# Attention and a routed expert layer on one core: scatter writes without mutual waits, weights in parts, reordered preparation

## The chip, the cores and the metric

The program runs on one core of a Trainium2 chip. The metric is the device time of one execution in microseconds (us). The core has five instruction streams that run side by side and wait for one another by semaphores: PE (TensorE, matrix products), DVE (VectorE), ACT (ScalarE), POOL (GpSimd) and SP (which here only issues transfers). Each stream executes its instructions in the order of the program, so an instruction that waits holds up everything behind it on the same engine. In the profile, PEld stands for the loading of weights into TensorE, and a name with q (SPq, POOLq) for the queue of that engine.

## What is computed

Attention over 8 batches, 12 heads, 448 tokens and head size 64, all in fp32, and behind it a layer in which only 128 of the 448 tokens of a batch, those with the highest gate score, go through two matrix products:

```
q_n, k_n = rmsnorm(q, g_q), rmsnorm(k, g_k)
attn = softmax(scale * q_n @ k_n.T)           # per batch and head
x = (attn @ v) with the heads side by side    # (8, 448, 768)
scores = x @ w_gate
out = x.copy()
for b in range(8):
    top = indices of the 128 highest scores[b]
    h = max(x[b, top] @ w1, 0)                # w1: 768 x 1024
    out[b, top] += sigmoid(scores[b, top]) * (h @ w2)
```

## The kernel before

**Tiling.** Four heads form a group; a batch has 3 groups, the whole problem 24. The 448 keys of a group are cut into 7 units of 64, so there are 168 units. `scores(u)` (L252) makes the transposed scores of a unit for 4 heads with 64x32 tiles of the array, and ACT turns them into probabilities `p` (L261), scaled by the keys' inverse norms `rinv`. `values(u)` (L278) multiplies them with `v` into two banks `av` that gather over the 7 units of a group. `add_probs` (L291, DVE) adds the probabilities up over the units; `sum_keys` (L315, `den`) and `invert_sums` (L331, `denT`, and a reciprocal on DVE) make the softmax's denominators from that sum. `values_out` (L303 on ACT, L305 on DVE) moves the finished `av` to SBUF as `xT`, and `to_tokens` (L345, L347), once for each pair of heads, turns it to token rows `x` and divides.

**Norms.** For each group ahead of its first unit: `squares` (ACT, L167) and `sum_squares` (DVE, L173) for the queries and the keys, `rinv` by a power on POOL (L177), then `rows_out` and `rows_in` (L190, L202): the queries' `rinv` goes to DRAM and comes back spread over the partitions as `bc`, with which `scale_q` (DVE, L211) scales the queries. Group 0 takes a way through TensorE instead (`scale_q_early`, L223).

**Selection and experts.** When a batch's 3 groups are done, `gate` (DVE, L368) makes the scores, `spread` and `score_rows` lay them out as rows, `count` (DVE, L401) gives each token its rank, `annotate` adds its gate and its row number, `select` (L433) writes the rows with rank under 128 to DRAM by four indirect transfers from POOL, and `load_selected` (L447, `xe`) reads them back. `mixture(b)` is a generator of 9 pieces: a head of transposes (L463), 4 pieces of the first product (L480), 4 half pieces of the second (L497, with L506 on DVE behind each half), and an indirect write of the rows at the end (L515, POOL).

**Order.** The program's order is written out by hand. The main loop goes in steps `k` of two units: scores of units 2k and 2k+1, values of the two units before, then what stands under slot 2k in a table `todo`, one piece of the running mixture, then slot 2k+1. A group that ends in step k has its `den` and `denT` in step k+1 and both `to_tokens` in step k+2; a batch has its `select` in the second half of step k+5, the load of `xe` in step k+6 and the head of its mixture in step k+8. 21 units make 10.5 steps, so the heads of successive mixtures stand 10 or 11 steps apart, and 9 of these steps carry a piece. All loads of inputs and weights, the `rows`/`bc` transfers, the store of `x` and the load of `xe` go through SP's one queue, in program order; a transfer there also waits until the eighth one before it has landed.

## Time and profile before

| | us |
|---|---|
| median of 3 runs | 658.07 (656.1 to 661.79) |
| profiled execution, device time | 659.13 |
| its span, first to last instruction | 657.4 |
| PE busy | 546.7 (83%) |
| DVE busy | 359.4 (55%) |
| ACT busy | 276.8 (42%) |
| POOL busy | 186.4 (28%) |
| mean granted TensorE clock | 0.928 of full |

The page shows the span of one execution, the busy time of each engine and, where asked, the rows of single instructions: start and duration in us, engine, line of the kernel, what it writes and reads, and in square brackets how long the engine had been idle and what ended that. A row with xN stands for N instructions of one kind in a run. A busy PE is not PE at its peak.

### The profile page before, as it was taken

How to read it: one execution, taken by the hardware profiler on the slowest of the kernel's cores; microseconds unless marked ns; L12 is line 12 of the kernel's file. 1: busy time of each engine (PE TensorE's matmuls, PEld its weight loads, DVE VectorE, ACT ScalarE, POOL GpSimd, SP SyncE). 2: the span in 40 equal slices, each digit the busy share in tenths (PEclk: the TensorE clock that was granted, in tenths of full speed). 3: DMA queues.
4: the chain of work that ended last, by engine and by line, in shares of the span. 5: the costliest groups of instructions: out<-in, count | busy, mean ns of one | idle time of the engine just before them, and what ended most of it. 6: DMA issues, size and time to landing. Idle time of an engine off the chain costs nothing.

```text
span 657.4 us, 15932 instructions
## 1 busy us (share of the span) xinstructions
PE 546.7 (83%) x6920; PEld 282.4 (43%) x6920; DVE 359.4 (55%) x588; ACT 276.8 (42%) x497; POOL 186.4 (28%) x99
## 2 busy tenths in 40 slices
PE   1638988689997999499996999599998999797185
PEld 1213333246434554156433654256435643284182
DVE  1446879554873568454873558554876476335000
ACT  1335665544544545444543544444544544410000
POOL 2633442511154223412053232512055212100200
PEclk9959998879997999979996999989999999798589
DMA  7975556172706534272806534273706331102200
GB/s 247 397 266 169 171 197 225 41 245 104 251 22 197 195 109 169 67 236 86 253 20 205 187 91 167 68 230 112 252 27 220 113 114 35 40 1 84 72 1 28
DMA packets 46914, 93.99 MB, mean 143 GB/s; under 512 B 11510, under 2 KB 29686, under 8 KB 46836
## 3 DMA queue, kind: packets, MB, share of 16 engines
q1 hardware_dynamic: 43492, 86.58, 39.9%
q0 software_dynamic: 3200, 6.31, 2.9%
q8 instruction: 56, 0.92, 0.6%
q14 instruction: 22, 0.18, 0.1%
q10 hardware_dynamic: 144, 0.00, 0.0%
HBM read 75.39 MB, written 25.36 MB: 153 GB/s over the span
## 4 chain that ended last, share of the span: by engine, by line
PE 53%; issue 21%; DMA 10%; POOL 7%; DVE 5%; ACT 3%; POOLq 0%; SPq 0%; DVEq 0%; ACTq 0%
PE sc L252 16%; PE av L278 13%; PE moe_ps L480 10%; PE moe_ps L497 7%; POOL selected L433 4%; DMA selected<-x,rank 4%; DMA xe<-selected 4%; PE x_ps L345 3%; DMA tok<-in_tok_dram 2%; POOL rinv L177 2%; ACT p L261 2%; DVE ss L173 2%; PE den_ps L315 1%; PE denT_ps L331 1%; DVE sum L291 1%
## 5 line engine op out<-in xcount | busy, mean ns | idle before, releaser
L261 ACT ACTIVATE p<-sc,rinv 128x448 f32<-128x448 f32 x336 | 186.5, 634 | 156.8 <-PE sc L252 141.2
L177 POOL TENSOR_TENSOR rinv<-ss,neg_half 128x14 f32<-128x14 f32 x48 | 136.7, 2848 | 300.6 <-DVE ss L174 280.2
L252 PE MATMUL sc<-qT,kT 64*32 64x448 f32 x2688 | 162.8, 588 | 15.9 <-ACT p L261 11.3
L278 PE MATMUL av<-p,v 64*32 64x448 f32 x2688 | 154.1, 556 | 7.3 <-ACT xT L303 7.3
L291 DVE TENSOR_TENSOR sum<-sum,p 128x896 f32<-128x896 f32 x120 | 129.3, 1077 | 4.7
L480 PEld LDWEIGHTS moe_ps<-xeT,w 128*128 128x128 f32 x768 | 90.5, 196 | 14.9 <-ACT p L261 11.0
L480 PE MATMUL moe_ps<-xeT,w 128*128 128x128 f32 x768 | 95.4, 282 | 1.5 <-ACT hT L487 1.5
L278 PEld LDWEIGHTS av<-p,v 64*32 64x32 f32 x2688 | 54.1, 111 | 90.1 <-issue 73.1
L497 PE MATMUL moe_ps<-w,hT 128*128 128x384 f32 x256 | 91.1, 502 | 1.9 <-DVE xe L506 1.4
L252 PEld LDWEIGHTS sc<-qT,kT 64*32 64x32 f32 x2688 | 46.6, 111 | 83.9 <-issue 60.6
L173 DVE TENSOR_REDUCE ss<-sq 128x14 f32<-128x896 f32 x48 | 51.9, 1080 | 35.1 <-ACT sq L167 35.1
L433 POOL DMA_INDIRECT selected<-x,rank x32 | 38.7, 1210 | 95.0 <-DVE x L426 46.6
L497 PEld LDWEIGHTS moe_ps<-w,hT 128*128 128x128 f32 x256 | 47.1, 193 | 41.7 <-issue 10.3
L347 DVE TENSOR_TENSOR x<-x_ps,rden 112x512 f32<-112x512 f32 x48 | 33.1, 690 | 40.5 <-PE x_ps L345 39.7
L167 ACT ACTIVATE sq<-tok 128x896 f32<-128x896 f32 x48 | 46.2, 962 | 14.8 <-DMA tok<-in_tok_dram 10.2
L487 ACT ACTIVATE hT<-moe_ps 128x256 f32<-128x256 f32 x32 | 12.3, 383 | 88.4 <-PE moe_ps L480 88.4
L345 PE MATMUL x_ps<-ident,xT 128*112 128x128 f32 x192 | 30.5, 281 | 11.9 <-DVE x L347 11.5
L463 PE MATMUL moe_ps<-ident,xe 128*128 128x128 f32 x24 | 6.5, 401 | 40.7 <-DMA xe<-selected 40.7
L506 DVE SCALAR_TENSOR_TENSOR xe<-moe_ps,xe 128x384 f32<-128x384 f32 x16 | 9.9, 618 | 53.2 <-PE moe_ps L497 53.1
L211 DVE SCALAR_TENSOR_TENSOR qT<-qT,gg,bc 128x896 f32<-128x896 f32 x23 | 26.4, 1148 | 17.3 <-DMA bc<-rows 17.3
L345 PEld LDWEIGHTS x_ps<-ident,xT 128*112 128x112 f32 x192 | 20.3, 133 | 32.7 <-DVE x L347 14.0
L305 DVE COPY xT<-av 128x448 f32<-128x448 f32 x24 | 15.0, 624 | 31.0 <-PE av L278 31.0
(54 smaller groups left out, 242.5 us busy)
## 6 DMA issues: line engine op xcount, KB each, us to landing
tok<-in_tok_dram SPq DMA_DIRECT2D x48, 448.0 KB, 6.5
qT<-in_qT_dram SPq DMA_DIRECT2D x24, 448.0 KB, 5.8
kT<-in_kT_dram SPq DMA_DIRECT2D x24, 448.0 KB, 7.6
v<-in_vp_dram SPq DMA_DIRECT2D x24, 448.0 KB, 7.6
out_dram<-x SPq DMA_DIRECT2D x8, 1344.0 KB, 7.3
bc<-rows SPq DMA_DIRECT2D x46, 224.0 KB, 4.0
w<-in_moe_w_dram SPq DMA_DIRECT2D x2, 3072.0 KB, 20.6
xe<-selected SPq DMA_DIRECT2D x8, 385.0 KB, 3.2
```

The costliest lines, as they stand in the source:

```text
L167: nc.scalar.activation(out=sq, in_=t, func=AF.Square, scale=scale)
L173: nc.vector.tensor_reduce(out=ss, in_=sq, axis=AX.X, op=OP.add)
L177: nc.gpsimd.tensor_tensor(out=rinv.rearrange(flat), in0=ss.rearrange(flat), in1=neg_half.to_broadcast([128, 2 * NI]), op=OP.pow,)
L252: nc.tensor.matmul(out=scs[hh][o : o + 32, 0:S], lhsT=kTs[n][r, c, D * i + k0 : D * i + k0 + 32], rhs=qTs[n][r, c, :], start=True, stop=True,)
L261: nc.scalar.activation(out=p[:, hh], in_=scs[hh][:, 0:S], func=AF.Exp, scale=rinvs[n, 1][:, hh, i : i + 1],)
L278: nc.tensor.matmul(out=avs[n][c][o : o + 32, 0:S], lhsT=vs[n][r, hh, i, d0 : d0 + 32], rhs=probs[u][r, hh], start=(i == 0), stop=(i == NI ...
L291: nc.vector.tensor_tensor(out=sums[n], in0=probs[u - 1] if i == 1 else sums[n], in1=probs[u], op=OP.add)
L345: nc.tensor.transpose(out=ps[:CP, j, :], in_=t[:, j, :], identity=ident)
L347: nc.vector.tensor_tensor(out=xs[b][:, :, col : col + 128].rearrange("p j (h d) -> p j h d", d=D), in0=ps[:CP].rearrange("p j (h d) -> p j ...
L433: nc.gpsimd.indirect_dma_start(out=t[:, :], out_offset=bass.IndirectOffsetOnAxis(ap=rank[:, j : j + 1], axis=0), in_=x[:, j, :], in_offset ...
L480: nc.tensor.matmul(out=ps[:, 128 * i : 128 * i + n], lhsT=w1[:, dc, 128 * (f0 + i) : 128 * (f0 + i + 1)], rhs=xeT[:, dc, :n], start=(dc == 0),
L497: nc.tensor.matmul(out=ps[:n, : DM // 2], lhsT=hT[:, fc, :n], rhs=w2[:, fc, cols], start=(fc == 0), stop=(fc == NFC - 1),)
```

## The change

- `select`: the four indirect writes of a batch are declared free of each other; each had waited for the one before.
- Weights: `w1` and `w2` had been loaded whole, right behind the first loads, ahead of the keys of group 1 and the tokens of group 2. They are now loaded in 14 parts, one in each slot from 8 to 21 (steps 4 to 10).
- Preparation: the first loads come in another order, those of group 1 among them; group 1's squares, sums and `rows`/`bc` transfers are issued ahead of the first scores; squares have two buffers; a small exponential ahead of everything loads ACT's table; the constant `earlier` is filled on POOL rather than on DVE and in step 4 rather than at the start.
- Queries come as (j, p) rather than (p, j) from the host, so that `values_out` and the copy of `den` read their bank straight; both copies of `values_out` are now on ACT.
- `sum_keys` makes its sums in four column tiles of 224 columns, where it had two of 448; the copy to `den` is 128x224 rather than 64x448, and `denT` takes two transposes rather than four.
- Order: a list of `tasks` is worked off at two places in a step, ahead of and behind the piece of the mixture. A group that ends in step q has `den` behind the piece of step q, `denT` ahead of that of q+1, the first `to_tokens` behind it, the second ahead of the piece of q+2. The first unit of a group is left to the next step where the group before it ends in this one.
- `gate` works per group on 256 columns (12 pieces for a batch, and a sum), where it had 4 pieces of 768 at the batch's end. `annotate` and `select` come in the first half of step q+5, ahead of the piece of the mixture; the load of `xe` too is in step q+5; the head stays in step q+8.
- The mixture's first product fills a whole bank before it is copied (two copies rather than four); the last batch's mixture takes the four banks of the scores, where it had one. `p` has 7 buffers rather than 6.

```diff
-    def load_weights():
-        nc.sync.dma_start(out=wg, in_=_bcast_row(moe_w_gate, CP))
-        nc.sync.dma_start(out=w1, in_=moe_w1.rearrange("(c p) f -> p c f", p=128))
-        nc.sync.dma_start(out=w2, in_=moe_w2.rearrange("(c p) f -> p c f", p=128))
+    def load_w(part):
+        if part == 0:
+            nc.sync.dma_start(out=wg, in_=_bcast_row(moe_w_gate, CP))
+        for w, src in ((w1, moe_w1), (w2, moe_w2)):
+            n = w.shape[1]
+            if part < n:
+                nc.sync.dma_start(
+                    out=w[:, part], in_=src.rearrange("(c p) f -> p c f", p=128)[:, part]
+                )
...
+            for odd in range(2):
+                o = 64 * odd + 32 * hh
+                nc.tensor.matmul(
+                    out=ps[o : o + 32, 0 : S // 2],
...
-            w = nc.gpsimd.indirect_dma_start(
+            for other in writes:
+                tc.declare_no_dep(w.ins, other.ins, reason="different rows")
+            writes.append(w)
...
+        def bank():
+            if b == B - 1:
+                return ps_sc.tile([128, 512], F32, name="sc")
+            return ps_moe.tile([128, 512], F32, tag="moe", name="moe_ps")
...
+    for part in range(NDC + NFC):
+        at(8 + part, load_w, part)
+    at(9, constants)
...
+        task((q, 1), sum_keys, n)
+        task((q, 2) if HALVES > 1 else (q + 1, 0), invert_sums, n)
+        task((q + 1, 0) if HALVES > 1 else (q + 1, 1), to_tokens, n, 0)
+        task((q + 1, 1) if HALVES > 1 else (q + 2, 0), last_tokens, n)
...
+        s = PER * (now[0] + 1)
+        at(s, count, b, (0, 1))
+        at(s + 1, count, b, (2, 3))
+        at(s + 2, annotate, b)
+        at(s + 2, select, b)
+        at(s + 3, load_selected, b)
+        ready.append((b, (s + 3) // PER + 4 // HALVES - 1))
```

(HALVES is 1 and PER is 2.)

Three places show what moves. The first is POOL's stream at the selection of the third batch: `selected` are the four indirect writes, `rinv` a norm ahead of them, and what a row waits for stands in brackets, where DMASW with a number is one of the eight completion semaphores that POOL's transfers take in turn, DMAHW the same for SP's, and the others stand for an engine. Before:

```order
L177 TENSOR_TENSOR rinv<-ss,neg_half 128x14 [waits DVE_49,Activation_49]
L433 DMA selected<-x,rank 128x770 [waits DVE_49]
L433 DMA selected<-x,rank 128x770 [waits DMASW3_49,DMASW2_49]
L433 DMA selected<-x,rank 128x770 [waits DMASW3_49]
L433 DMA selected<-x,rank 128x770 [waits DMASW4_49]
```

And of the change:

```order
L191 TENSOR_TENSOR rinv<-ss,neg_half 128x14 [waits DMAHW3_49,DMAHW4_49,DVE_49,Pool_49]
L454 DMA selected<-x,rank 128x770 [waits DMASW1_49,DVE_49]
L454 DMA selected<-x,rank 128x770 [waits DMASW2_49]
L454 DMA selected<-x,rank 128x770 [waits DMASW3_49]
L454 DMA selected<-x,rank 128x770 [waits DMASW4_49]
```

Before, the semaphore is that of the write just ahead; in the change each write takes the semaphore that a write of an earlier batch had used eight transfers back, and waits for that one alone.

The second place is SP's stream from its first load on. Before, with `w_143` and `w_144` for the two weights:

```order
L91 DMA tok<-in_tok_dram 128x896
L91 DMA qT<-in_qT_dram 128x2x448
L91 DMA tok<-in_tok_dram 128x896
L91 DMA kT<-in_kT_dram 128x2x448
L91 DMA v<-in_vp_dram 128x896
L91 DMA tok<-in_tok_dram 128x896 x2
L91 DMA qT<-in_qT_dram 128x2x448
L158 DMA wg<-in_moe_w_gate_dram 112x768
L159 DMA w_143<-in_moe_w_dram 128x6x1024
L160 DMA w_144<-in_moe_w_dram 128x8x768
L91 DMA kT<-in_kT_dram 128x2x448
L91 DMA v<-in_vp_dram 128x896
```

And of the change:

```order
L92 DMA tok<-in_tok_dram 128x896 x2
L92 DMA qT<-in_qT_dram 128x2x448
L92 DMA kT<-in_kT_dram 128x2x448
L92 DMA tok<-in_tok_dram 128x896 x2
L92 DMA v<-in_vp_dram 128x896
L92 DMA qT<-in_qT_dram 128x2x448
L92 DMA kT<-in_kT_dram 128x2x448
L92 DMA v<-in_vp_dram 128x896
L204 DMA rows<-rinv 64x2x7 x2
L216 DMA bc<-rows 64x2x448 x2
L92 DMA tok<-in_tok_dram 128x896 x2
```

The weights are gone from the start; the last row, the tokens of group 2, now stands behind the `rows` and `bc` of group 1, which wait for POOL.

The third place is PE's stream around the end of the second group, where no mixture runs. Before:

```order
L315 MATMUL den_ps<-sum,pick_pair 32x448 x2
L331 MATMUL denT_ps<-ident,den 112x64 x4
L252 MATMUL sc<-qT,kT 32x448 x16
L278 MATMUL av<-p,v 32x448 x16
L345 MATMUL x_ps<-ident,xT 112x128 x8
L252 MATMUL sc<-qT,kT 32x448 x16
```

And of the change:

```order
L327 MATMUL den_ps<-sum,pick_pair 32x224 x4
L266 MATMUL sc<-qT,kT 32x448 x16
L292 MATMUL av<-p,v 32x448 x16
L345 MATMUL denT_ps<-ident,den 112x128 x2
L359 MATMUL x_ps<-ident,xT 112x128 x4
L266 MATMUL sc<-qT,kT 32x448 x16
L292 MATMUL av<-p,v 32x448 x16
L359 MATMUL x_ps<-ident,xT 112x128 x4
```

Scores and values now stand between `den` and `denT` and between the two `x_ps`, which share one bank.

## Rows read from the trace of the kernel before

**Rows 1.** Stretches: length, busy time (instructions) per engine, granted clock, DMA share, GB/s.
```profile
20.00:40.00 20.00, 8.65 (x145) 3.83 (x144) 5.62 (x10) 8.28 (x14) 9.57 (x8) 0.86 1.04 400
50.50:124.70 74.20, 61.86 (x1036) 23.59 (x1028) 56.03 (x86) 45.93 (x80) 28.04 (x12) 0.95 0.50 168
55.50:86.60 31.10, 26.95 (x488) 10.49 (x480) 23.70 (x31) 20.68 (x36) 13.22 (x4) 1.00 0.45 147
132.70:567.20 434.50, 397.08 (x5148) 204.07 (x5148) 263.08 (x426) 203.68 (x369) 128.50 (x63) 0.95 0.45 144
495.80:567.20 71.40, 65.95 (x890) 33.87 (x890) 43.30 (x69) 33.06 (x61) 17.92 (x9) 1.00 0.36 114
567.20:621.80 54.60, 36.42 (x262) 23.45 (x262) 17.16 (x38) 6.61 (x14) 4.72 (x5) 0.81 0.15 48
```

**Rows 2.** Waits: engine, line, releaser: total us, times, longest us.
```profile
PE moe_ps L463 <- DMA xe<-selected: 40.7, 8, 14.1
```

**Rows 3.** Timeline of PE at two heads of a mixture.
```profile
270.08 1.72 PE L252 MATMUL sc<-qT,kT 64*32 64x448 f32 x32
...
273.23 0.95 PE L315 MATMUL den_ps<-sum,pick_pair 128*32 128x448 f32 x4
279.35 0.91 PE L463 MATMUL moe_ps<-ident,xe 128*128 128x128 f32 x3 [5.17 <-DMA xe<-selected]
...
282.06 3.24 PE L252 MATMUL sc<-qT,kT 64*32 64x448 f32 x32
...
291.28 1.74 PE L252 MATMUL sc<-qT,kT 64*32 64x448 f32 x32
...
555.23 0.65 PE L345 MATMUL x_ps<-ident,xT 128*112 128x128 f32 x4 [0.78 <-DVE x L347]
...
559.65 0.99 PE L278 MATMUL av<-p,v 64*32 64x448 f32 x16 [1.35 <-ACT xT L303]
...
567.21 0.90 PE L463 MATMUL moe_ps<-ident,xe 128*128 128x128 f32 x3 [2.69 <-DMA xe<-selected]
```

**Rows 4.** The tile selected: issue on POOL, ns min/median/max; then landing.
```profile
L433 POOL DMA_INDIRECT selected<-x,rank x32: 940/943/2407, 117.4 to 615.6; - x32
...
DMA to landing us min/median/max: 2.5/2.9/5.0
```

**Rows 5.** Timeline of POOL at the last selection.
```profile
606.57 0.94 POOL L433 DMA_INDIRECT selected<-x,rank  x1 [44.16 <-DVE x L426]
...
615.58 0.94 POOL L433 DMA_INDIRECT selected<-x,rank  x1 [2.04 <-DMA selected<-x,rank]
616.82 0.96 POOL L515 DMA_INDIRECT out_dram<-xe,row  x1 [0.30 <-issue]
```

**Rows 6.** Timeline of DVE and ACT in the opening stretch.
```profile
17.50 1.08 DVE L173 TENSOR_REDUCE ss<-sq 128x14 f32<-128x896 f32 x1
...
37.70 0.95 ACT L167 ACTIVATE sq<-tok 128x896 f32<-128x896 f32 x1 [10.24 <-DMA tok<-in_tok_dram]
...
44.79 1.15 DVE L211 SCALAR_TENSOR_TENSOR qT<-qT,gg,bc 128x896 f32<-128x896 f32 x1 [2.70 <-DMA bc<-rows]
```

**Rows 7.** DMA issues: queue, count, KB each, median us from issue to landing.
```profile
tok<-in_tok_dram SPq DMA_DIRECT2D x48, 448.0 KB, 6.5
...
rows<-rinv SPq DMA_DIRECT2D x46, 3.5 KB, 2.7
```

**Rows 8.** Timeline of DVE at the last batch's ranks.
```profile
601.61 0.62 DVE L506 SCALAR_TENSOR_TENSOR xe<-moe_ps,xe 128x384 f32<-128x384 f32 x1 [5.04 <-PE moe_ps L497]
```

**Rows 9.** Groups by line: busy us, mean ns, idle before.
```profile
L177 POOL TENSOR_TENSOR rinv<-ss,neg_half 128x14 f32<-128x14 f32 x48 | 136.7, 2848 | 300.6 <-DVE ss L174 280.2 <-issue 8.5 <-DMA v<-in_vp_dram 7.2
...
L480 PE MATMUL moe_ps<-xeT,w 128*128 128x128 f32 x768 | 95.4, 282 | 1.5 <-ACT hT L487 1.5
...
L368 DVE SCALAR_TENSOR_TENSOR prod<-x,wg 112x768 f32<-112x768 f32 x32 | 30.6, 955 | 0.8
...
masks.py:197 POOL MEMSET ident<- 128x128 f32 x1 | 0.2, 204 | 3.9 <-DVEq L1084 3.9
```

More of the change, by code (lines that the diff above doesn't have):

```diff
@@ new lines, in run_values @@
+    def run_values(upto, q):
+        ended = False
+        while waiting and waiting[0] <= upto:
+            u = waiting[0]
+            if ended and u % NI == 0:
+                return
+            values(waiting.pop(0))
+            if u % NI == NI - 1:
+                values_out(u // NI)
+                finish(u // NI, q)
+                ended = True
+            add_probs(u)
+    sq = {}
+    sq[0, 0] = squares(0, 0)
+    sum_squares(0, 0, sq.pop((0, 0)))
+    sq[0, 1] = squares(0, 1)
@@ new lines, in fast @@
+    sum_squares(0, 1, sq.pop((0, 1)))
+    sq[1, 0] = squares(1, 0)
+    sq[1, 1] = squares(1, 1)
+    scale_q_early(0)
+    sum_squares(1, 0, sq.pop((1, 0)))
+    rows_out(1)
+    sum_squares(1, 1, sq.pop((1, 1)))
+    rows_in(1)
+    waiting = list(range(units))
+    moe, ready, done, q = iter(()), [], 0, 0
+    while done < B:
+        now[0] = q
+        for half in range(HALVES):
+            k = 2 * (HALVES * q + half)
+            for u in (k, k + 1):
+                if u < units:
+                    scores(u)
+            run_values(k - 1, q)
+            for slot in (k, k + 1):
+                for fn in todo.pop(slot, ()):
+                    fn()
+        opening(q, 0)
+        for half in range(HALVES):
+            end = next(moe, None)
+            if end is None and ready and q >= ready[0][1]:
+                moe = mixture(ready.pop(0)[0])
+                end = next(moe)
+                done += 1
+            opening(q, half + 1)
+            if end and HALVES > 1:
+                break
+        q += 1
```

206 lines of the change are left out of this document (94 added, 112 removed).

## The prediction

> **What bounds the kernel now.** I read the stretches first, then the waits, then the single rows at the places that the two name. The span falls into four parts: up to the head of the first mixture at 132.7 us; six batches from there to 567.2, 434.5 us; the last batch's way to its selected rows, 54.6 us; and its mixture, 35.6 us, from 621.8 to the end at 657.4 [rows 1]. In the third of these that is clean, 495.8 to 567.2, PE is busy 65.95 of 71.4 us at a granted clock of 1.00, and DVE 43.30: with a mixture running, PE is the bound. Where it isn't busy, the waits name one cause above all: the first transpose of a mixture waits for `xe`, 40.7 us in 8 waits, the longest 14.1 [rows 2]; the other seven make 26.6, 3.8 each. Behind such a wait PE pays again: after 5.17 us of waiting the scores of two units take 3.24 us, where 1.74 is the time a few steps later [rows 3], the two clock levels of 1.2 and 2.4 GHz. The opening is another thing: there one square on ACT sits 10.24 us for tokens that stand behind both weights in SP's queue [rows 6].
>
> **The change, part by part.**
>
> **The opening.** With the weights away, the tokens of group 2 wait for something else: SP has the `rows` and `bc` of group 1 ahead of them, and `rows` needs POOL. DVE gets to the sum for group 1's queries at about 17.0 (17.50 in [rows 6], less half a microsecond for the table that is loaded earlier); 1.2 for the sum and its small follower, 2.8 for the power [rows 9], 2.7 for `rows` to land and 6.5 for `bc` and tokens behind it [rows 7] make 30.2, where the square started at 37.70. That is 7.5 us. The wait of 2.70 for group 1's `bc` [rows 6] goes too, since it is issued ahead of those tokens: 10.2 in all.
>
> **Attention without a mixture.** From 55.5 to 86.6 seven steps take 31.1 us, 4.44 each, with PE busy 26.95 and DVE 23.70 [rows 1]. The new order puts scores and values between `den` and `denT` and between the two `x_ps`. PE's work falls by what four column tiles save: `den` takes 0.95 now [rows 3]; halved columns on twice the tiles can save from nothing to half, and I take 0.4 for each of the two groups. DVE loses two copies to ACT, whose 20.68 of 31.1 has room for them, and gains eight pieces of `gate`: a piece of 768 columns takes 0.955 [rows 9], one of 256 between a third of that and all of it; I take 0.5, near the third since the work is by column, which makes DVE about 26.5. So both engines end near 26.3, 3.8 a step at the least; with both that full I take 4.1, half way to 4.44. The stretch from 50.5 to 124.7 holds 15 steps in 74.2 us [rows 1]; now 61.5, plus 3 for the first batch's ranks on DVE: 64.5, a gain of 9.7.
>
> **Weights in the middle.** They are 6.3 MB in seven steps, some 29 us, beside two groups' loads of 2.7 MB each: 12 MB. From 20 to 40 us the queues moved 400 GB/s [rows 1], so 30 us are needed; I add 2 us for loads that come late. The Trainium skill, DMA: Bandwidth & Descriptors, section "Where 436 GB/s comes from", gives about 358 GB/s as the limit of HBM for one core; by that these loads would need 33.5 us, and the sum would be 3 us longer. The row has 400, and the measurement decides.
>
> **The writes of selected rows.** From the first to the last issue are 9.0 us now, 606.57 to 615.58, three turns of 3.0, of which the issue itself is 0.94 and the rest the landing of the write ahead; the next transfer behind the last of them, which waited for none of these, came 1.24 after it [rows 5]. Four issues in a row so take 3.7 from first to last, 5.3 less. In the middle batches there is a second gain: `select` comes ahead of the mixture's piece, most of a step earlier, and a step is 71.4 / 11 = 6.5 us: some 5. The write's landing, 2.9, and the load of `xe` remain. Together about 10 us against waits of 3.8 (longest of the seven 5.17) and a head that itself comes some 3 us earlier: the seven waits go. The Trainium skill, SBUF — State Buffer, section "SBUF: two separate sides", speaks against this: POOL cannot write descriptors while certain DVE instructions hold the port pair that both share. The rows show something of it, 943 ns at the median and 2407 at most for one issue [rows 4]. With four at the most, first to last would be 3 x 2.7 = 8.1, and the sum below would be longer by 4.4 at the first and at the last batch, while in the batches between the earlier place covers it. I stay with 3.7 and leave the 8.1 to a rival.
>
> **A batch behind its head.** The clean batch, 11 steps, takes 71.4 [rows 1]. Off it come the wait at its end, 2.69, the values' wait for the copies of `av`, 1.35, the second `x_ps`, 0.78 [rows 3], and 3 x 0.4 of `den`: 65.4. A batch of 10 steps lacks one bare step of 3.15 (270.08 to 273.23 [rows 3]): 62.2. Three of each are 382.8. I add 1.5 a batch for waits that the new order may bring, since `den`, `denT`, both `x_ps`, the score rows and half of the head still share one bank, and since SP, blocked at `xe`, holds the next `bc`: 391.8, against 434.5.
>
> **The end.** Of the 54.6 us [rows 1], the writes give 5.3; `count` stood behind the mixture's output on DVE, which sat 5.04 us for PE [rows 8], and now stands ahead of it; I take 4.3 of the 5.04, since the transposes and the copy of the score rows still come first; and without a wait at 567.21 scores and values there run at the high clock, about 2.5 by the 1.5 of [rows 3] for the scores and one more for the values. That leaves 42.5. The last mixture, with four banks, waits less for its copies: PE waited 1.5 us in all for them [rows 9]; 35.6 becomes 34.1.
>
> **At nothing.** `earlier` on POOL: a fill of 128 columns takes 0.204 there [rows 9], so 1792 take up to 2.9, and behind four selects DVE's small copy waits for it, up to 5 us once. What hides it is work that is ahead at that point: the scores and probabilities of the next units need nothing of DVE's next rows; without that cover it costs those 5. One buffer more for `p`, two for squares and two large copies of the product's output move nothing on a path that I see; they could give a microsecond or two at the opening.
>
> **The sum.** First part: 132.7 - 10.2 - 9.7 - 3.8 + 2 = 111.0. With 391.8, 42.5 and 34.1 the span is 579.4, against 657.4. The profiled execution took 659.13, 1.7 more than its span, and lies 1.1 above the median of 658.07; so 580 us against that median, 12% less.
>
> **The rivals.**
>
> *Half the wait stays.* The issues stretch, as the most in [rows 4] allows, or a semaphore that the writes share holds them; the order shows that each waits only for one eight transfers back, which speaks against it. Half of 3.8 and some 2.5 of low clock, seven times, make 31: 610 us.
>
> *The opening stays long.* SP's queue is in order, and `rows`, `bc` and tokens come one behind the other with POOL in between; if DVE's wait for the constants and the bunched loads add up, I lose 14 us of the first part: 594.
>
> *The new order fits better than I grant.* No waits of 1.5 a batch, 3.8 a step: 9 and 4.5 less, 566 us. For it speaks that PE is busy 65.95 of 71.4 us in the clean batch [rows 1], so that little else than the named waits stands there.
>
> *Slower.* One thing could do it: the granted clock. If TensorE, with hardly a pause for 400 us, were granted the low level, its work would take 3.24 for 1.74 [rows 3], 1.86 times as long. From 580 to 665 are 85 us: it decides if about 100 us of PE's work, a fifth, run at the low level. Against it: from 495.8 to 567.2 PE is busy 92% at 1.00 [rows 1], and every low stretch that I looked at follows a pause. And with no effect at all: the waits that PE shows would have to be covered by other ones of the same length, for which I see no row.
>
> **How the numbers follow.** My forecast, 568 to 592, has a chance of 0.55; half the wait 0.13, the long opening 0.15, the better fit 0.13, slower 0.02, no effect 0.02. The likeliest gives 580. The range of 556 to 608 takes in the better fit, the long opening and the lower half of "half the wait stays", and the bounds of `den` (10 us for 24 groups) and of the loads. A measurement of this kernel can tell about 1% from no change; faster by more than that 0.96, within it 0.02, slower 0.02.
>
> **What would show it.** Right: PE's wait for `xe` under 15 us in all and most of that at the last batch; four `selected` issued within 4 to 5 us; the first head near 111; heads 62 and 65 us apart; granted clock near 1.00 between. Wrong: heads over 68 apart, which means that the bank or `bc` took the place of `xe`; the square of group 2 still starting past 35; attention steps above 4.4, DVE then being full; POOL's issues near 2.4 each.

## The result and the profile after

The changed kernel takes 605.29 us (median of 4 runs, 603.63 to 613.48), against 657.95 for the kernel before on the same chip: a ratio of 0.918, with an interval of 0.913 to 0.924. The run of 613.48 was 1.6% slower than the fastest, at a lower granted clock (0.94 where the other three had 0.95), and the ratio leaves it out. The forecast was 580, the range 556 to 608. So the direction was right and the time lies near the upper end of the range, 25 us above the likeliest. The profiled execution of the changed kernel took 604.48 us, with a span of 602.8. By the four parts of the prediction, from the profiled spans:

| part of the span, us | before | predicted | after |
|---|---|---|---|
| start to the first mixture head | 132.7 | 111.0 | 127.3 |
| first to seventh head (six batches) | 434.5 | 391.8 | 402.7 |
| seventh to eighth head | 54.6 | 42.5 | 41.4 |
| eighth head to the end | 35.6 | 34.1 | 31.3 |
| sum | 657.4 | 579.4 | 602.8 |

The last two parts came out as worked out, or better, by 3.9 us together. The miss of 23.4 us is in the first part (16.3) and in the six batches (10.9), less these 3.9. The stretches of the trace after, in the columns of [rows 1]: 15 steps of attention, the six batches, the last of these, and the last batch.

```profile
43.08:123.16 80.08, 64.03 (x1036) 23.65 (x1020) 56.01 (x107) 45.09 (x82) 32.82 (x19) 0.88 0.73 250
127.35:530.08 402.73, 381.07 (x5187) 202.18 (x5186) 260.81 (x510) 205.30 (x376) 141.43 (x64) 0.97 0.47 154
462.53:530.08 67.55, 65.12 (x899) 35.04 (x898) 42.73 (x83) 33.86 (x63) 19.58 (x9) 1.00 0.35 115
530.08:571.46 41.38, 31.30 (x263) 21.34 (x261) 16.16 (x47) 6.42 (x13) 4.74 (x5) 0.98 0.20 63
```

Fifteen steps of attention took 74.2 us before [rows 1] and take 80.1 now, at a granted clock of 0.88: this stretch became slower, where the prediction had 64.5. The six batches have PE busy 381 of 403 us; in the last of them, 67.6 long, it is busy 96% of the time.

The waits (engine, line, releaser: total us, times, longest us):

```profile
PE xeT_ps L488 <- DVE row L498: 17.2, 6, 5.7
DVE qT L225 <- DMA bc<-rows: 14.6, 4, 5.5
PE moe_ps L488 <- DMA xe<-selected: 6.0, 1, 6.0
```

PE's wait for `xe`, 40.7 us in 8 [rows 2], is down to one of 6.0 at the last batch. But a few rows behind the place where it stood there is a new one, 17.2 us in 6: the second half of a mixture's transposes. What it waits for is seen at the third head, in the timelines of PE, DVE and SP, one fence each (start, duration, instruction, and in brackets the idle time ahead of it and what ended it):

```profile
256.51 0.43 PE L345 MATMUL denT_ps<-ident,den 128*112 128x128 f32 x2
256.78 0.49 PE L488 MATMUL moe_ps<-ident,xe 128*128 128x128 f32 x3
262.96 0.90 PE L488 MATMUL xeT_ps<-ident,xe 128*128 128x128 f32 x3 [5.69 <-DVE row L498]
...
265.46 3.24 PE L266 MATMUL sc<-qT,kT 64*32 64x448 f32 x32
```

```profile
261.59 1.15 DVE L225 SCALAR_TENSOR_TENSOR qT<-qT,gg,bc 128x896 f32<-128x896 f32 x1 [5.53 <-DMA bc<-rows]
262.65 0.25 DVE L347 RECIPROCAL rden<-denT_ps 112x16 f32<-112x16 f32 x1
262.82 0.10 DVE L498 CAST row<-xe 128x1 int32<-128x1 f32 x1
```

```profile
230.11 0.61 SPq L92 DMA_DIRECT2D v<-in_vp_dram  x1
252.00 0.33 SPq L472 DMA_DIRECT2D xe<-selected  x1
252.43 1.53 SPq L204 DMA_DIRECT2D rows<-rinv  x2
256.97 1.24 SPq L216 DMA_DIRECT2D bc<-rows  x2
```

They read from the bottom up. SP issues nothing between 230.7 and 252.0, since the load of `xe` stands next in its queue and waits for the writes of the selected rows. `rows` and `bc` of the next group stand behind it. So `bc` lands at about 261.5; DVE sits 5.53 us for it ahead of `scale_q` (L225); the reciprocal `rden` stands behind `scale_q` on DVE, and until it has read `denT`, the one bank `ps_aux` isn't free for the second half of the head. PE sits 5.69 (the view names the small copy `row`, which DVE ends 0.02 us behind `rden`), and the scores behind take 3.24 instead of 1.73 at 246.25 (1.74 before, [rows 3]), the low one of the two clock levels. The prediction named this as a sign of failure ("the bank or `bc` took the place of `xe`"), but had 1.5 us a batch for it.

The four writes are now issued one behind the other. The tile `selected` after:

```profile
L454 POOL DMA_INDIRECT selected<-x,rank x32: 938/1001/2321, 112.4 to 565.1; - x32
```

At the first batch they start at 112.41, 113.86, 115.11 and 116.36, which is 3.95 from first to last. At the third, where one issue took 2.32, it is 5.17, the most of the eight batches; at the last it is 3.75.

In the stage of attention the same chain shows, with the weights in SP's queue in the place of `xe`. SP, DVE and PE there:

```profile
72.10 1.25 SPq L204 DMA_DIRECT2D rows<-rinv  x2
...
80.43 1.24 SPq L216 DMA_DIRECT2D bc<-rows  x2
```

```profile
84.87 1.15 DVE L225 SCALAR_TENSOR_TENSOR qT<-qT,gg,bc 128x896 f32<-128x896 f32 x1 [3.56 <-DMA bc<-rows]
```

```profile
86.25 1.10 PE L359 MATMUL x_ps<-ident,xT 128*112 128x128 f32 x4 [3.41 <-DVE rden L347]
87.28 3.24 PE L266 MATMUL sc<-qT,kT 64*32 64x448 f32 x32
```

From `rows` to `bc` 8.3 us pass, where the opening needs 3.1 (22.01 to 25.11): `rows`, 3.5 KB, takes up to 8.1 us to land here, where its median before was 2.7 [rows 7].

### The profile page after: what moved, and what is told of

The parts are those of the page before. It is cut to its first block, busy times and chain, and to the rows that moved or that the text cites. A ratio compares the mean times of both kernels' runs of the same rounds, so it can differ in the third digit from the quotient of the medians.

```text
span 602.8 us, 16209 instructions
## 1 busy us (share of the span) xinstructions
PE 525.2 (87%) x6968; PEld 277.8 (46%) x6968; DVE 354.3 (59%) x699; ACT 278.9 (46%) x506; POOL 198.0 (33%) x100
## 4 chain that ended last, share of the span: by engine, by line
PE 58%; issue 13%; DMA 10%; DVE 8%; POOL 4%; ACT 3%; SPq 3%; DVEq 0%; POOLq 0%
PE sc L266 17%; PE av L292 13%; PE moe_ps L511 11%; PE moe_ps L530 10%; PE x_ps L359 4%; DMA rows<-rinv 3%; DMA bc<-rows 3%; POOL rinv L191 2%; DMA tok<-in_tok_dram 2%; DVE sum L305 2%; ACT p L275 2%; DVE ss L187 2%; PE den_ps L327 1%; DMA v<-in_vp_dram 1%; SPq L92 1%
## 5 line engine op out<-in xcount | busy, mean ns | idle before, releaser
L191 POOL TENSOR_TENSOR rinv<-ss,neg_half 128x14 f32<-128x14 f32 x48 | 145.5, 3033 | 293.2 <-DVE ss L188 237.3
L266 PE MATMUL sc<-qT,kT 64*32 64x448 f32 x2688 | 160.0, 577 | 8.5 <-ACT p L275 8.5
L511 PE MATMUL moe_ps<-xeT,w 128*128 128x128 f32 x672 | 80.6, 277 | 0.0
L511 PEld LDWEIGHTS moe_ps<-xeT,w 128*128 128x128 f32 x672 | 77.2, 192 | 7.3 <-issue 5.1
L530 PE MATMUL moe_ps<-w,hT 128*128 128x384 f32 x224 | 78.2, 493 | 2.2 <-DVE xe L539 1.5
L454 POOL DMA_INDIRECT selected<-x,rank x32 | 38.9, 1215 | 71.1 <-DVE x L446 63.2
L530 PEld LDWEIGHTS moe_ps<-w,hT 128*128 128x128 f32 x224 | 40.4, 190 | 33.1 <-issue 5.1
L385 DVE SCALAR_TENSOR_TENSOR prod<-x,wg 112x256 f32<-112x256 f32 x96 | 40.6, 423 | 2.5
L359 PEld LDWEIGHTS x_ps<-ident,xT 128*112 128x112 f32 x192 | 21.3, 139 | 39.7 <-DVE sum L305 14.6
L305 DVE TENSOR_TENSOR sum<-p 128x896 f32<-128x896 f32 x24 | 26.1, 1087 | 20.2 <-ACT p L275 20.2
L225 DVE SCALAR_TENSOR_TENSOR qT<-qT,gg,bc 128x896 f32<-128x896 f32 x23 | 26.4, 1147 | 14.6 <-DMA bc<-rows 14.6
L421 DVE SCALAR_TENSOR_TENSOR cmp<-score_rows,gate,earlier 112x448 f32<-112x448 f32 x32 | 21.9, 684 | 10.8 <-ACT score_rows L412 10.1
L520 ACT ACTIVATE hT<-moe_ps 128x512 f32<-128x512 f32 x14 | 8.4, 598 | 39.5 <-PE moe_ps L511 39.5
## 6 DMA issues: line engine op xcount, KB each, us to landing
w<-in_moe_w_dram SPq DMA_DIRECT2D x6, 512.0 KB, 10.9
```

The costliest lines, as they stand in the source:

```text
L191: nc.gpsimd.tensor_tensor(out=rinv.rearrange(flat), in0=ss.rearrange(flat), in1=neg_half.to_broadcast([128, 2 * NI]), op=OP.pow,)
L266: nc.tensor.matmul(out=scs[hh][o : o + 32, 0:S], lhsT=kTs[n][r, c, D * i + k0 : D * i + k0 + 32], rhs=qTs[n][r, c, :], start=True, stop=True,)
L305: nc.vector.tensor_tensor(out=sums[n], in0=probs[u - 1] if i == 1 else sums[n], in1=probs[u], op=OP.add)
L359: nc.tensor.transpose(out=ps[:CP, j, :], in_=t[:, j, :], identity=ident)
L385: nc.vector.scalar_tensor_tensor(out=prod, in0=xs[b][:, j, cols], scalar=1.0, in1=wg[:, cols], op0=OP.mult, op1=OP.mult, accum_out=gates[b ...
L454: w = nc.gpsimd.indirect_dma_start(out=t[:, :], out_offset=bass.IndirectOffsetOnAxis(ap=rank[:, j : j + 1], axis=0), in_=x[:, j, :], in_of ...
```

## The experiments

Each kernel ran together with the kernel before on one chip, whose median there lay between 658 and 662 us; ratios are to it, and "the changed kernel" has 0.918. What is said of single stretches is from the run's own trace, with its own line numbers.

**1. The writes wait again.** Theory: the wait for `xe` was the largest item of the kernel before, and the declaration alone takes it away. Edit to the changed kernel:

```diff
-            for other in writes:
-                tc.declare_no_dep(w.ins, other.ins, reason="different rows")
```

> The changed kernel, in which only the four writes of selected rows wait for one another again. Theory of the prediction (the waits for xe were worth the most of the change): from the first to the last of four issues it takes 9 us again instead of 4 to 5, so xe comes some 4.5 us later at each head; at the middle heads it had about 1.3 us to spare, so PE waits some 3 us for xe at six heads, SP is held at xe's load for 4.5 us longer and the next group's bc comes that much later too, and the low clock behind a wait costs 1.5 to 2.5 each; with 5 us at the last batch some 35 to 40 us more than the changed kernel's 605: 640, a ratio of 0.97 to the kernel before. Rival (the earlier place of the selection alone covers the writes): only the last batch's 5 us and a few more, 610 to 615, a ratio of 0.93.

Measured: 633.2 us, ratio 0.959 (0.952 to 0.966), so 27 us more than the changed kernel; between the two expectations, nearer to the theory. Its waits:

```profile
POOL selected L454 <- DMA selected<-x,rank: 48.1, 24, 2.6
DVE qT L225 <- DMA bc<-rows: 35.1, 6, 11.0
PE moe_ps L485 <- DMA xe<-selected: 26.0, 8, 11.2
```

The writes wait 2 us each for the one ahead, PE waits 26.0 for `xe` again, and the wait for `bc` grows from 14.6 to 35.1, since SP is held longer at `xe`. The chain is one: the later `xe`, the later `bc`.

**2. The kernel before with that declaration alone.**

```diff
+            for other in writes:
+                tc.declare_no_dep(w.ins, other.ins, reason="different rows")
```

> The kernel before, with nothing changed but that the four writes of selected rows don't wait for one another. Theory of the prediction: 5.3 us at the last batch, and at the seven other heads, where PE waits 3.8 us for xe in the mean, most of that and 1.5 to 2.5 us of low clock behind it: 5 us each, in all some 40, so 618 us, a ratio of 0.94. Rival (in the old order the selection is late because DVE's ranks are late, and another wait takes xe's place): the last batch's 5 us and little more, 645 to 650, a ratio of 0.985.

Measured: 621.8 us, ratio 0.943 (0.938 to 0.947), as the theory had it. Its heads lie at 128.20 and 537.26 (first and seventh), 409.1 apart where the kernel before has 434.5. PE's wait for `xe` is left at the last batch alone:

```profile
PE moe_ps L467 <- DMA xe<-selected: 8.8, 1, 8.8
```

So in the old order the declaration clears the seven other waits without the earlier place of the selection. Of the 52.7 us that the change brings, this declaration alone brings 38. And its first head, 128.20, is 0.9 us from that of the changed kernel, 127.35: all the rest of the change together gained 0.9 us up to there, where the prediction had 17.9 (10.2 + 9.7 - 2).

**3. All weights at once behind the opening.**

```diff
-    for part in range(NDC + NFC):
-        at(8 + part, load_w, part)
...
     rows_in(1)
+    for part in range(NDC + NFC):
+        load_w(part)
```

> The changed kernel with all fourteen parts of the weights issued at once, behind the loads of the opening and the rows of group 1, instead of one in each half step from the fourth step on. Theory L (the loads of the weights in the stage of attention made bc late there and cost most of the 16 us by which the first head came later than forecast): the square of group 2 starts 6 to 9 us later, past 39, but the bc waits of that stage go and 15 steps take 65 to 70 us where they took 80; first head at 120 to 125, 598 to 603 us in all. Rival D (DVE's rows and the order of the work are late by themselves): the steps stay at 78 to 80 us and the first head comes 6 to 9 us later, near 135, 611 to 615 us in all.

Measured: 624.6 us, ratio 0.944 (0.939 to 0.949), 17 us more than the changed kernel; worse than either theory. ACT in the opening:

```profile
48.78 0.95 ACT L181 ACTIVATE sq<-tok 128x896 f32<-128x896 f32 x1 [24.00 <-DMA tok<-in_tok_dram]
```

The square of group 2 starts at 48.78, not past 39 as expected: the tokens stand behind all the weight loads. Then the 15 steps take 74.9 us instead of 80.1, so theory L is right in kind, but the loads in parts cost only some 5 of the 16 us by which the first head came late; and the later opening costs more than that gives back.

**4. The load of `xe` from POOL's queue.**

```diff
-        nc.sync.dma_start(out=xe[:CAP], in_=slots_dram.pop(b))
+        nc.gpsimd.dma_start(out=xe[:CAP], in_=slots_dram.pop(b))
```

> The changed kernel with the load of xe issued by POOL instead of SP, so that SP is not held at it while it waits for the writes of the selected rows. Theory Q (rows and bc stand behind the held load in SP's queue; the late bc holds the scaling of the queries on DVE, with the inverted sums behind it, and these hold the one bank that the mixture's second half of xeT needs): the wait of PE at that half, 17.2 us in 6, falls to under 5, above all the two of 5.69 and 4.67, and with the low clock behind them 12 to 18 us go: 587 to 593. Rival (DVE is late by its own load, bc or no bc): the waits at that half stay above 12 us and the time within 1% of 605. Where POOL, held at the load in SP's stead, now brings the powers late, the waits of POOL's followers would grow and the gain fall under 10 us.

Measured: 603.3 us, ratio 0.916 (0.910 to 0.922), not told apart from the changed kernel. The wait at the second half of the head is gone, as theory Q says (0.20 at the first head, none in the next two), and DVE's wait for `bc` falls from 14.6 us in 4 to 3.0 in one. But:

```profile
PE moe_ps L488 <- DMA xe<-selected: 20.2, 7, 6.7
```

The wait moved to `xe`: at the third head the load leaves POOL at 250.81, 6.0 us after the last of the four issues had ended, behind a power of 2.62 us and 3.37 us of waiting, where SP let it go 1.7 us after the last issue had ended. The power is POOL's own order; what the 3.37 us were is not shown (the trace puts them down to PE's values). That the late `bc` comes from SP being held at `xe` is shown by this run, a gain isn't.

**5. The preparation two steps earlier.** This takes the other way: `xe` stays on SP, and what stood behind it is put ahead.

```diff
-            prepare(n, s0 - 12)
-            at(0 if n == 2 else max(s0 - 20, 5), load_tok, n, 0)
-            at(0 if n == 2 else max(s0 - 20, 5), load_tok, n, 1)
+            prepare(n, s0 - 12 if n < 4 else s0 - 16)
+            at(0 if n == 2 else max(s0 - 24, 5), load_tok, n, 0)
+            at(0 if n == 2 else max(s0 - 24, 5), load_tok, n, 1)
```

> The changed kernel with the squares, powers, rows and bc of each group from the fifth on issued four half steps (two steps) earlier, and their tokens as much earlier, so that rows and bc stand ahead of xe's load in SP's queue. Theory Q (SP, held at xe's load, makes bc late, and the late bc makes DVE late at the heads; late bc also holds the steps of the attention stage): PE's wait at the mixture's second half of xeT, 17.2 us in 6, falls under 5 without new waits for xe, DVE's wait for bc, 14.6 in 4, under 3; 15 to 22 us less than the changed kernel: 583 to 590, ratio 0.885 to 0.895. Rival (as in the run with xe's load on POOL, the wait moves on to xe or to the sums, since DVE and ACT are late by themselves): within 1% of 605, ratio 0.91 to 0.925.

Measured: 577.5 us, ratio 0.874 (0.869 to 0.879): 28 us less than the changed kernel, more than theory Q expected, and the best of all. PE's wait at the second half of the head, and the stretches (15 steps, and six batches):

```profile
PE xeT_ps L488 <- DVE row L498: 0.7, 3, 0.2
```

```profile
41.85:113.86 72.01, 58.93 (x1037) 22.55 (x1021) 57.26 (x109) 47.90 (x86) 36.90 (x20) 0.94 0.80 278
119.25:503.26 384.01, 374.06 (x5185) 198.47 (x5185) 257.52 (x506) 204.46 (x374) 135.99 (x62) 1.00 0.49 159
```

PE's wait at the second half falls from 17.2 to 0.7 us, DVE's wait for `bc` vanishes from the list, and the six batches take 384.0, with PE busy 97% of it at a granted clock of 1.00. The first head comes at 119.25 instead of 127.35. The earlier place gives 18.7 us in the six batches and 8.1 ahead of them.

**6. The weights' parts in every second half step.**

```diff
-        at(8 + part, load_w, part)
+        at(8 + 2 * part, load_w, part)
```

> The changed kernel with the fourteen parts of the weights issued in every second half step (until 34) and not in each (until 21). Theory L (the loads bunched between 50 and 80 us, 378 and 367 GB/s there, make rows and bc take 8.3 us from issue to issue and so hold the attention stage): DVE's wait of 3.56 for bc at 85 us goes, and the x_ps wait of 3.41 behind it; first head 6 to 8 us earlier, 597 to 600 us in all. Rival (the steps are late by DVE and the new order): first head at 126 to 128 and 603 to 607 us.

Measured: 606.8 us, ratio 0.919 (0.913 to 0.924), no change. The first head does come 6.0 us earlier, at 121.33, as theory L has it, but the six batches take 411.9 instead of 402.7, with 23.2 us of waits at the second half of the head instead of 17.2. The waits are 6.0 of the 9.2 us by which the batches are longer. Why they came out longer there isn't settled.

**7. The kernel before with the declaration and the weights in parts.** As run 2, with `load_w` as in the change, and

```diff
-    load_weights()
...
+    for part in range(NDC + NFC):
+        at(8 + part, load_w, part)
```

> The kernel before with two parts of the change: the writes of selected rows don't wait for one another, and the weights come in fourteen parts, one in each half step from the fourth step on. Without the weights' part its first head stood at 128.2 us and the time at 621.8. Theory O (the new order of sums, tokens and preparation itself costs some 10 us up to the first head, and the weights' parts gain 10 in either order): first head at 116 to 120, 608 to 613 us. Rival N (the late weights gain only where rows and bc of group 1 stand ahead of the tokens of group 2, that is in the new opening): first head at 125 to 130, 617 to 623 us.

Measured: 608.9 us, ratio 0.922 (0.917 to 0.928): the time that theory O gave, and not told apart from the changed kernel. Its first head is at 124.91, though, where theory O had 116 to 120, so its reason holds by half. Two parts of the change, in the old order of work, make a gain that can't be told from the whole one.

**8. Two column tiles for the sums again.**

```diff
-            for odd in range(2):
-                o = 64 * odd + 32 * hh
...
+            nc.tensor.matmul(
+                out=ps[32 * hh : 32 * (hh + 1), 0:S],
+                lhsT=pick_pair,
+                rhs=sums[n][:, hh],
...
```

The copy to `den` (64x448) and the four transposes of `denT` go back with it.

> The changed kernel with the sums over keys in two column tiles of 448 as before instead of four of 224. Theory of the prediction (PE is the bound, and the four tiles save 0.36 us for each of 24 groups; ACT's copy and the transposes take as long as before or a little less): 8 to 9 us more, 613 to 615, ratio 0.931. Rival (PE's saving falls into waits for DVE and ACT, since den comes just ahead of a wait for them): 603 to 608, ratio 0.915 to 0.923.

Measured: 616.5 us, ratio 0.931 (0.925 to 0.938), as the prediction's theory had it. The matrix products of the sums, first in this kernel, then in the changed one (count, ns min/median/max):

```profile
L325 PE MATMUL den_ps<-sum,pick_pair x96: 536/540/564, 45.1 to 559.3; 128*32 128x448 f32 x96
```

```profile
L327 PE MATMUL den_ps<-sum,pick_pair x192: 349/353/378, 46.2 to 543.5; 128*32 128x224 f32 x192
```

A group's products span 0.95 us in two tiles [rows 3] and 0.59 in four, which is 8.6 us over 24 groups. The time moved by 1.3% of 660, 8.4, in which the two intervals leave some 6 us either way. So the saving on the fullest engine shows in the time, and its size agrees; that it arrived whole is more than these intervals can tell.

**9. Run 5 with two more edits**, the weights as in run 6 and the copy of the token numbers eight steps later:

```diff
-        nc.vector.tensor_copy(out=token_f, in_=token_i)
+    at(24, constant_copy)
```

> The run with the preparation two steps earlier (577 us), with two more edits: the weights' parts in every second half step, and DVE's small copy of token numbers, which sat 4.03 us for POOL at 46 us, eight steps later. Theory (in the stage of attention DVE is now the fullest engine, 57.3 of 72.0 us, so that what it sits for there costs time, and rows to bc still takes 7 to 9 us where weights stand between): the copy gives 3 to 4 us, the sparser weights 2 to 4, first head at 112 to 115 instead of 119, 570 to 573 us. Rival (as with the sparser weights alone, what is won ahead of the first head is given back in the batches, or DVE's 4 us were ahead of work that PE had in store): 575 to 579.

Measured: 579.3 us, ratio 0.877 (0.873 to 0.881), no gain over run 5; first head at 119.91. With two edits at once the time can't tell one from the other, but the trace shows the cover of DVE's 4 us: without the copy DVE sits 2.87 us at that place for probabilities from ACT, and PE's next wait for DVE is 0.51 us where run 5 has 1.01. The rival holds.

**10. Run 7 with the preparation two steps earlier**, the edit of run 5 in the old order:

```diff
-        prepare(n, *((1, 1) if n == 1 else (s0 - 12, 2)))
+        prepare(n, *((1, 1) if n == 1 else (s0 - 12 if n < 4 else s0 - 16, 2)))
...
```

> The kernel before with three things: the writes of selected rows don't wait for one another, the weights come in parts in the fourth to the tenth step, and squares, powers, rows, bc of each group from the fifth on come two steps earlier. It leaves out the new order of work, the queries as (j, p), the four column tiles and the gate by pieces. Theory S (with bc early the change's remaining parts are worth 15 to 25 us: four column tiles some 8, the copies of den and the product without a stride and the places between scores and values the rest): 592 to 602 us. Rival T (bc was what mattered, and the remaining parts give their 8 us of column tiles at most): 580 to 588 us. Third (the old order has other waits, so an early bc does nothing there): 605 to 612.

Measured: 627.0 us, ratio 0.950 (0.947 to 0.952), 18 us more than run 7 and outside all three expectations. Every batch of 11 steps takes 74 to 75 us where run 7 has 68.5 to 70; those of 10 steps take 64 in both. At the end of one of 11 steps, on DVE and on PE:

```profile
253.91 0.69 DVE L355 TENSOR_TENSOR x<-x_ps,rden 112x512 f32<-112x512 f32 x1 [3.19 <-remote]
```

```profile
254.66 0.65 PE L353 MATMUL x_ps<-ident,xT 128*112 128x128 f32 x4 [3.88 <-DVE x L355]
255.24 3.23 PE L260 MATMUL sc<-qT,kT 64*32 64x448 f32 x32
```

DVE sits 3.19 us ahead of the first rows of the next batch, while POOL issues the selected rows (247.8 to 253.0), PE waits for it and pays the low clock. There are three such waits, 10.8 us in all, one in each batch of 11 steps; in run 7 DVE writes the same rows at 248.32 without a wait, 0.23 us after POOL's first issue. The trace names the releaser only as "remote", and what it is stays open. What the run shows for sure: the earlier preparation is no gain by itself; it pays 28 us in the new order and costs 18 in the old one.

**11. The preparation one step earlier.** The edit of run 5 with `s0 - 14` and `s0 - 22`. By the order of SP's queue `bc` then stands ahead of `xe` at the first, third and fifth head, and behind it at the second, fourth and sixth.

> The changed kernel with the preparation of each group from the fifth on one step earlier instead of two. In SP's queue rows and bc then stand ahead of xe's load at the first, third, fifth and seventh batch, while at the second, fourth and sixth rows stands ahead of it and bc behind it. Theory Q: the waits of PE at the second half of xeT go at the first, third and fifth head (1.30, 5.69 and 4.67 us in the changed kernel) and stay, at 1 to 6 us, at the second, fourth and sixth; 588 to 597 us. Rival (what counted in the run with two steps was the earlier start of the powers and squares, not the place in SP's queue): the waits shrink at all six heads alike, or at none.

Measured: 593.7 us, ratio 0.898 (0.896 to 0.901). The six heads:

```profile
123.18 0.55 PE L488 MATMUL xeT_ps<-ident,xe 128*128 128x128 f32 x3 [0.34 <-DVE row L498]
186.62 0.55 PE L488 MATMUL xeT_ps<-ident,xe 128*128 128x128 f32 x3 [2.39 <-DVE row L498]
255.49 0.55 PE L488 MATMUL xeT_ps<-ident,xe 128*128 128x128 f32 x3 [0.34 <-DVE row L498]
318.90 0.55 PE L488 MATMUL xeT_ps<-ident,xe 128*128 128x128 f32 x3 [2.38 <-DVE row L498]
387.99 0.55 PE L488 MATMUL xeT_ps<-ident,xe 128*128 128x128 f32 x3 [0.34 <-DVE row L498]
451.43 0.55 PE L488 MATMUL xeT_ps<-ident,xe 128*128 128x128 f32 x3 [2.41 <-DVE row L498]
```

And SP ahead of the first and of the second:

```profile
107.66 1.24 SPq L216 DMA_DIRECT2D bc<-rows  x2
118.16 0.35 SPq L472 DMA_DIRECT2D xe<-selected  x1
```

```profile
177.10 0.34 SPq L472 DMA_DIRECT2D xe<-selected  x1
177.56 1.26 SPq L216 DMA_DIRECT2D bc<-rows  x2
```

Where `bc` stands ahead of `xe` the wait is 0.34, where it stands behind, 2.4, head by head as theory Q says. An earlier start alone would have shortened all six alike. With runs 4 and 5 this settles the cause of the new wait. Most of the 16 us to run 5 lie in the three batches behind these longer waits: 70 to 71 us each, where run 5 has 65 to 67.

**12. Run 5 with ACT's table loaded first.**

```diff
+    neg_half = const.tile([128, 1], F32, name="neg_half")
+    nc.vector.memset(neg_half, -0.5)
+
+    warm = const.tile([128, 1], F32, name="warm")
+    nc.scalar.activation(out=warm, in_=neg_half, func=AF.Exp)
+
     gcol = const.tile([128, 2], F32, name="gcol")
     nc.scalar.dma_start(out=gcol, in_=g2)
...
```

(These lines stood behind `gg`.)

> The run with the preparation two steps earlier (577 us), with the fill of neg_half and the first exponential set ahead of the load of the constants gcol, so that ACT's table load, which stood at 8.07 us behind DVE's wait for gcol, starts at about 4.5. Theory (the prediction's own: the table stands ahead of the first square, so half a microsecond to a whole one goes from the opening): the first square, at 9.47, starts at 8.2 to 8.9, the first scores, at 17.36, up to 1 us earlier, 576 us, a difference that the times hardly tell. Rival (the first square waits for the tokens' transfer, and the first scores for v's, as the wait of 14.5 us before L237 says): table at 4.5 and square and scores within 0.3 us of where they were, 577 us.

Measured: 578.6 us, ratio 0.874 (0.872 to 0.877), the same as run 5. The table load in the changed kernel, and in this one with the first square:

```profile
8.03 1.28 ACT L132 ACT_TABLE_LOAD   x1 [8.03 <-DVE pick_pair L135]
```

```profile
4.58 1.28 ACT L126 ACT_TABLE_LOAD   x1 [4.58 <-DVE neg_half L123]
...
7.63 0.95 ACT L181 ACTIVATE sq<-tok 128x896 f32<-128x896 f32 x1 [1.56 <-DMA tok<-in_tok_dram]
```

In the changed kernel the "earlier" table load isn't early: its input is filled by DVE behind the wait for `gcol`. Put right, the first scores start at 16.33 instead of 17.36, the microsecond that the theory has, and the fourth step at 40.80 instead of 41.85; the first head at 120.61 shows nothing of it any more.

## Why the prediction was right or wrong, point by point

**The wait for `xe`, right.** That PE waits under 15 us for it, and at the last batch alone, is what the trace after shows (6.0, once). Runs 1 and 2 bear the price out: 27 us when it is put back, 38 when it alone is taken away. Issues of 1.2 us at the mean (38.9 us for 32) are nearer to the row's 0.94 than to its 2.4; the page SBUF — State Buffer of the Trainium skill, section "SBUF: two separate sides", allows for stretched issues, and single ones of 2.3 do occur, but first to last stayed between 3.75 and 5.17 in the eight batches, against 3.7 forecast and 8.1 in the rival; no run shows that DVE is what stretches them. For the seven middle waits I had counted on the earlier place of the selection as well; run 2 shows that the declaration alone was enough in the old order, and run 1 that the earlier place without it leaves 26.0 us in 8 waits where there were 40.7.

**A batch behind its head, right in kind, its allowance mis-sized.** "I add 1.5 a batch ... since SP, blocked at `xe`, holds the next `bc`" was the step that failed. Six batches lost 402.7 - 391.8 = 10.9 more than that, 3.3 a batch in place of 1.5. The order showed that `bc` stands behind `xe`, `scale_q` behind `bc`, `rden` behind `scale_q` and half of the head behind `rden`; I had each link and didn't work out how long the chain gets: SP let go at 252.0, 9.6 us for `rows` and `bc`, 1.2 for the scaling. Of the 19.9 us above the bare 382.8, 17.2 are PE's wait at the second half of the head. The heads lie 62.3 to 69.8 us apart, two of the six over the 68 that I had named as a sign of this. Run 5 takes the chain away and measures 384.0, even 7.8 less than the forecast, near the rival "fits better", which asked for 9 us less.

**The attention stage, wrong.** "With both that full I take 4.1" is the term that failed. Over the 15 steps 5.3 a step were measured, worse than the 4.9 before. The seven steps from which I took the term, 55.5 to 86.6 before [rows 1], are these after, and in run 5:

```profile
46.68:78.49 31.81, 26.37 (x489) 10.38 (x485) 26.35 (x46) 22.95 (x42) 14.20 (x6) 1.00 0.94 336
```

```profile
45.36:76.07 30.71, 26.37 (x488) 10.38 (x484) 27.55 (x48) 24.03 (x43) 15.05 (x7) 1.00 0.82 287
```

That is 4.54 and 4.39 a step, at the high clock, where 4.44 stood before. PE and DVE are as busy as I had worked out (near 26.3 both), so the work was right, and the overlap was wrong: I took half of the idle time off without a reason for it. PE still sits 5.4 us there, all of it for the sums and reciprocals of DVE, and 4.3 in run 5; before it sat 4.2, of which 2.6 were for copies on ACT. The new order took those waits away and put others in their place. The larger loss is in the seven steps behind these: 44.7 us (78.49 to 123.16), where they took 38.1 before and I had 31.7. There `bc` is late behind the weights: with all the weights ahead of it (run 3), with half as many a step (run 6) or with the preparation earlier (run 5) these seven steps take 37.8, 37.7 and 37.8, so the weights between `rows` and `bc` cost 6.9 us. Of the 6 that are left above 31.7, most stand at the first batch's ranks. In the trace of run 5, on PE, stands

```profile
93.25 0.97 PE L408 MATMUL row_ps<-ident,spread 112*112 112x112 f32 x4 [4.91 <-DVE spread L401]
94.15 3.24 PE L266 MATMUL sc<-qT,kT 64*32 64x448 f32 x32
```

which is a wait of 4.91 us for the spread scores and the low clock behind it; the 3 us that I had for the ranks don't hold that. In the 72.0 us of run 5's 15 steps PE is idle 13.1, and 12.5 of these it waits for DVE, which is busy 57.3. That DVE's chain of sums, tokens, gate and ranks sets the pace there is read from these waits; no run takes work off it.

**The opening, mis-sized.** The chain through `rows`, `bc` and tokens is the one that I worked out. The square of group 2 started at 32.99, not at 30.2, and the fourth step at 43.08 where it was at 50.50 [rows 1]: 7.4 us of the 10.2. Of the 2.8 us by which the square is late, 1.0 is the sum of group 1's queries (18.04, not 17.0) and 1.4 the issue of `bc` on SP ahead of the tokens (25.11 to 26.47), which I had put at nothing. What I had for an earlier table load didn't come, since it wasn't earlier (run 12).

**The weights in the middle, mis-sized.** I had 2 us of loss, and their gain in the opening; the loss was 6.9, as told above. As a whole the parts are worth 17 us in the new order (run 3, against all at once behind the opening) and 13 in the old (runs 2 and 7, against whole loads at the start). In the trace after, the two fullest stretches of ten microseconds, in the columns of [rows 1], are

```profile
50.00:60.00 10.00, 8.60 (x154) 3.21 (x138) 8.53 (x13) 6.79 (x13) 6.56 (x2) 1.00 1.03 378
70.00:80.00 10.00, 8.19 (x164) 3.23 (x164) 9.47 (x17) 7.91 (x15) 3.95 (x1) 1.00 0.96 367
```

which is less than the 400 GB/s that I reckoned with. It is more than the 358 that the Trainium skill gives as the HBM limit per core (DMA: Bandwidth & Descriptors, "Where 436 GB/s comes from"), but nearer to it. What came late and held the stage was not the weights, though, but the small `rows` between them (up to 8.1 us to land) and `bc` behind it. Whether the one queue or the loads as such delay `rows` is not shown, since no run gave it another queue.

**The column tiles, right.** 0.4 us a group forecast, 0.36 measured, and run 8 finds 8.4 us of it in the time, to some 6 us.

**The end, right, its four banks mis-sized.** 41.4 for 42.5, and 31.3 for 34.1: the last mixture is 4.3 shorter, where I had granted its four banks 1.5. No run tests the banks by themselves.

**At nothing, right.** DVE's copy did wait for POOL (4.04 us), and the trace of run 9 shows that it had cover.

**The rivals and the range.** "Half the wait stays" comes closest in time, 610, and that is chance: the wait for `xe` went, and another took its place. "The opening stays long", 594, names the right part of the span, but most of the loss there was behind the opening: 2.8 us in it, 15.6 in the attention stage. The clock didn't decide: 0.95 over the span, and in the trace after the scores that take over 3 us stand behind a wait of PE. That 605 lies within the range is in part luck: the range reached to 608 for rivals whose causes did not come, and the narrower 568 to 592 was missed.

**What the parts are worth.** The declaration and the weights' parts alone give 608.9 (run 7), the whole change 605.3. The column tiles in it are worth 8.4, so the rest of the reordering gave nothing, or cost some 5; each of these differences is known to some 6 us only. With `bc` early the same reordering gives 577.5, while the old order then takes 627.0. The parts don't add up; that this comes from SP's queue and the one bank, which they share, is shown for `bc` in the new order (runs 5 and 11) and open for the old one (run 10).

## What to carry to other kernels

When a wait is taken away, follow the next resource that the waiting instruction held: here the load that waits for the rows sits at the head of an in-order queue, and what is queued behind it becomes the new wait. Put transfers whose inputs are ready ahead of a transfer that has to wait, and if the chain behind it can be named (queue, landing, engine, bank), add its links up instead of giving it an allowance. Small transfers that others depend on come late between bulk loads: look at where they stand in the queue before the bulk loads are moved. And take idle time off a stretch only where the wait that makes it is known to go.

## What the runs showed of the hardware

The same edit, an earlier preparation, gained 28 us in one order of the work and lost 18 in another. In the changed kernel a wait of PE of 3.4 to 5.7 us cost about 1.5 more by the low clock level behind it on the scores alone (3.24 for 1.73), and up to 1.0 on the values behind them (2.69 for 1.71 at 90.27 us), at `bc` just as at `xe` before. `rows`, 3.5 KB, took up to 8.1 us to land while the weights ran at 367 GB/s, where its median before was 2.7. And moving a load to another engine's queue (run 4) didn't free it: it left that queue 6.0 us after the last write's issue had ended, where SP let it go after 1.7, and PE's wait for `xe` grew from 6.0 us in one to 20.2 in 7.
